# Keys and values of neighbouring units in one load of 64 KB rows

## The chip, the core and the metric

The kernel runs on one core of a Trainium2 chip. The metric is the device time of one execution in microseconds (us), the median of the runs shown. Sizes: 1 MB of a load is 1,048,576 bytes, as the profile counts KB by 1,024; the profile's MB and GB/s are decimal.

## The reference

Two rounds of the same two layers work on one token for each of two batch rows. A layer of attention reads a cache of 4,096 keys and values for 16 heads, and a gated feed-forward layer follows. Everything is float32.

```
B, D, H, Sk, Dh, F = 2, 448, 16, 4096, 256, 1792
def A(x):                                   # attention over the cache
    q = (x @ wq), split into heads          # [B, H, 1, Dh]
    scores = einsum("bhqd,bhkd->bhqk", q, k_cache) * Dh**-0.5
    p = softmax(scores)
    o = einsum("bhqk,bhkd->bhqd", p, v_cache)
    return o, heads joined, @ wo
def F(x):                                   # feed-forward
    gate = x @ W_gate; up = x @ W_up
    return (gate * (gate > 0) * up) @ W_down
x = x + A(layernorm(x)); x = x + F(layernorm(x))
x = x + A(layernorm(x)); x = x + F(layernorm(x))
```

Both rounds use the same weights and the same cache. The cache is 2 x 16 x 4,096 x 256 x 4 bytes, 134 MB for the keys and as much for the values, and it is read once in each round.

## The kernel before, in words

A **unit** is one head of one batch row: 32 units in a pass, and a pass is the attention of one round. A unit's keys are 4,096 rows of 256 floats. They lie on 128 partitions with 32 rows (32 KB) on each, and so do its values. One quarter of that, 8 rows (8 KB) on each partition, 1 MB in all, is a **chunk**; a unit has four chunks of keys and four of values.

All loads go through one arena in SBUF, 27 places of a chunk's size. The first 24 are six blocks of four (`BLOCKS`, line 25), three are single places, mostly for the weights of a head ("h": query weights and output weights, 896 KB) and of the feed-forward layer ("in", "out"). `Arena.take` (line 42) chooses free places: for a load of four chunks the first block that is wholly free, for a single chunk a place that splits no free block.

The order of the loads is a list made before anything runs. `loads` (line 142) puts for each unit the keys, then the values of the unit before, and after each second unit the weights of the next head. `grouped` (line 157) makes one load of 4 MB out of four chunks in mid-pass, with rows of 32 KB; the last 12 entries of a pass (`ENDS`) and the first 25 of the second (`SMALL`) stay single chunks of 1 MB with rows of 8 KB. The first pass goes through the units forwards, the second backwards, so that what is loaded last in the first pass can stay for the second (`keep`, line 171: 20 chunks, one more and one head). `pump` (line 111) takes loads from the head of the list as long as `take` finds a place and issues them at line 125 from the sync engine SP; `release` (line 135) gives a place back and calls `pump`. As the list is strict, a load that finds no place holds up all behind it, and SP takes its waits in that order.

What is done with the data of unit u, in the loop of line 502:

- VectorE multiplies the keys with the query in two halves (`score_block`, line 364, 4,096 elements a partition each) and sums most of them up (line 373); ScalarE sums the first chunk (line 369). All four chunks of the keys are released behind that. Units kept for the second pass go by line 405, chunk by chunk, and so do units 0 to 4 of the second pass, with line 396.
- GpSimd takes the maximum over the partitions (line 416), ScalarE makes the exponentials (line 424).
- In the next turn of the loop TensorE weighs the values (`weigh`, line 443, 32 matmuls a unit) and releases them chunk by chunk. Ahead of it in TensorE's program stand the output projection of the unit pair before (`project`, line 486, which releases the head's weights) and, in odd units, the query of the next pair (`query`, line 323).

So turn u of the loop reads the keys of u and the values of u - 1.

Of the kernel before, what the change touches and what calls it, by code (L numbers as in the profile page):

```python
# [8 lines left out]
F32 = mybir.dt.float32  # L9
# [5 lines left out]
B, D, H, S, DH, F = 2, 448, 16, 4096, 256, 1792  # L15
P = 128
DC = 5
FULL, TAIL = 3, 64
NT = S // P
CT = 8  # L20
UNIT = CT * DH
NC = NT // CT
BLOCKS, SINGLES = 6, 3
KEPT = 20

SUMS = 96
# [9 lines left out]
class Arena:  # L36


    def __init__(self):
        self.free = set(range(BLOCKS * NC + SINGLES))  # L40

    def take(self, n, kind, after=None):

        blocks = [range(NC * i, NC * i + NC) for i in range(BLOCKS)]
        whole = [r for r in blocks if all(k in self.free for k in r)]
        split = {k for r in whole for k in r}
        if n > 1:
            found = [r[0] for r in whole]  # L50
        else:
            found = sorted(self.free, key=lambda k: (k in split, k))
            if kind in "kv":
                found = [k for k in found if k < BLOCKS * NC]
                if after is not None and after % NC != NC - 1 and after + 1 in found:
                    found = [after + 1]
            else:
                single = [k for k in found if k >= BLOCKS * NC]
                found = single if kind == "h" else single + found
        if not found:  # L60
            return None
        self.free -= set(range(found[0], found[0] + n))
        return found[0]
# [3 lines left out]
def two_layers(  # L67
    ctx: ExitStack,
    tc: tile.TileContext,
    x: bass.AP,  # L70
    k_cache: bass.AP,
    v_cache: bass.AP,
    w_head: bass.AP,
    w_in: bass.AP,
    w_out: bass.AP,
# [5 lines left out]
    consts = ctx.enter_context(tc.tile_pool(name="consts", bufs=1))  # L81
# [4 lines left out]
    ps_a = ctx.enter_context(tc.tile_pool(name="ps_a", bufs=1, space=PSUM))  # L86
    ps_f = ctx.enter_context(tc.tile_pool(name="ps_f", bufs=2, space=PSUM))

    arena = consts.tile([P, (BLOCKS * NC + SINGLES) * UNIT], F32, name="arena")
    ctx.enter_context(tc.manual_schedule())  # L90


# [3 lines left out]
    at_of = {}  # L96
    blocks = set()

    def source(key, n):
        kind, name, c = key  # L100
        if kind in "kv":
            h, b = name
            rows = (k_cache if kind == "k" else v_cache)[b, h]
            return rows.rearrange("(p t) d -> p (t d)", t=NT)[:, c * UNIT : (c + n) * UNIT]
        if kind == "h":
            return w_head[name]
        if kind == "in":
            return w_in[c]
        return w_out[:, 14 * P * c : min(14 * P * (c + 1), 14 * D)]

    def pump():
        while pending:
            (kind, name, c), n = pending[0]
            last = at_of.get((kind, name, c - 1)) if kind in "kv" else None
            at = units.take(n, kind, last)
            if at is None:
                return
            pending.pop(0)
            src = source((kind, name, c), n)
            dst = arena[:, at * UNIT : at * UNIT + src.shape[1]]  # L120
            parts = [0, src.shape[1]]
            if not pending:
                parts[1:1] = [src.shape[1] - CLOSE * TAIL]
            for i, j in zip(parts, parts[1:]):
                nc.sync.dma_start(dst[:, i:j], src[:, i:j])
            for k in range(n):
                at_of[kind, name, c + k] = at + k
            if n == NC:
                blocks.add((kind, name))

    def get(*key):
# [3 lines left out]
    def release(*key):  # L135
        units.free.add(at_of.pop(key))
        pump()

    first = [(h, b) for h in range(H) for b in range(B)]
    second = first[::-1]  # L140

    def loads(order):
        found = [("h", order[0][0], 0)]
        for u, unit in enumerate(order):
            found.append(("k", unit, 0))
            if u > 0:
                found.append(("v", order[u - 1], 0))
            if u % 2 and u + 1 < len(order):
                found.append(("h", order[u + 1][0], 0))
        return found + [("v", order[-1], 0)]  # L150

    def cut(found):

        for kind, name, c in found:
            yield from ((kind, name, c + k) for k in range(NC if kind in "kv" else 1))

    def grouped(keys, begin, end):

        keys = list(keys)
        found, i = [], 0  # L160
        while i < len(keys):
            kind, name, c = keys[i]
            whole = kind in "kv" and c == 0 and begin <= i and i + NC <= len(keys) - end
            found.append((keys[i], NC if whole else 1))
            i += found[-1][1]
        return found

    ffn_loads = [("in", "", c) for c in range(7)] + [("out", "", c) for c in range(4)]
    of_first, of_second = list(cut(loads(first))), list(cut(loads(second)))

    keep = {of_second[0], *[key for key in of_second if key[0] != "h"][:KEPT]}
    keep.add(("v", second[2], NC - 1))
    of_second = [key for key in of_second if key not in keep]

    heads = [key for key in of_second if key[0] == "h"][:2]
    of_second = [key for key in of_second if key not in heads]
    of_second[NC - 1 : NC - 1] = heads
    pending += grouped(of_first, 0, ENDS) + [(key, 1) for key in ffn_loads]
    pending += grouped(of_second, SMALL, ENDS) + [(key, 1) for key in ffn_loads]

    row = consts.tile([P, 2 * DH], F32, name="row")
    down = consts.tile([P, D], F32, name="down")
    junk = down[:, :DH]
    y_end_row = row[SUMS : SUMS + B, D:]
    nc.scalar.dma_start(row[:B, :D], x.rearrange("b s d -> (b s) d"))
    pump()


# [557 lines left out]
    found = out.rearrange("b s d -> (b s) d")  # L746
# [11 lines left out]

def _arrays(np, A_x, A_k_cache, A_v_cache, A_wq, A_wo, B_W_gate, B_W_up, B_W_down, **_):

    rows = FULL * P
    wq = A_wq.reshape(D, H, DH)
    head = [wq[c * P : (c + 1) * P].transpose(1, 0, 2) for c in range(FULL)]
    head.append(wq[rows:].reshape(TAIL, H, 2, P).transpose(1, 2, 0, 3).reshape(H, P, P))
    wo = A_wo.reshape(H, 2, P, D)
    head += [wo[:, 0], wo[:, 1]]
    full = [w[c * P : (c + 1) * P] for w in (B_W_gate, B_W_up) for c in range(FULL)]
    full.insert(FULL, np.concatenate([B_W_gate[rows:], B_W_up[rows:]]))
    down = B_W_down.reshape(4, D, D)
    chunks = [down[j, m * P : (m + 1) * P] for j in range(4) for m in range(FULL)]  # L770
    chunks += [np.concatenate([down[j, rows:], down[j + 1, rows:]]) for j in (0, 2)]
    found = {
        "x": A_x,
        "k_cache": A_k_cache,
        "v_cache": A_v_cache,
        "w_head": np.concatenate(head, axis=2),
        "w_in": np.stack(full),
        "w_out": np.concatenate(
            [c[:, at : at + P] for at in range(0, D, P) for c in chunks], axis=1
        ),  # L780
    }
    return {n: np.ascontiguousarray(a) for n, a in found.items()}


def build(nc, shapes):
    import concourse.tile as _tile

    args = [
        nc.dram_tensor(f"in_{n}_dram", s, F32, kind="ExternalInput").ap() for n, s in shapes.items()
    ]  # L790
    for i, (shape, _) in enumerate(_OUTS):
        args.append(nc.dram_tensor(f"out_{i}_dram", shape, F32, kind="ExternalOutput").ap())
    with _tile.TileContext(nc) as tc:
        two_layers(tc, *args)
# [12 lines left out]
```

## Time and profile before

| | |
|---|---|
| runs (us) | 1330.64, 1327.22, 1329.90; median 1329.9 |
| span of the profiled execution, first to last instruction | 1325.7 us |
| median less the profiled span | 4.2 us |
| VectorE busy | 1004.0 us, 76% |
| TensorE busy, matmuls | 581.5 us, 44% |
| ScalarE, GpSimd busy | 325.1 us, 106.2 us |
| moved by all queues | 563.20 MB, 425 GB/s on average |

The profile shows one execution. Its span does not hold what lies ahead of the first and behind the last instruction; the profiled execution's own time isn't listed apart from its span, so the span is set against the median of the three runs.

How to read the rows that follow: a row of a timeline has its start, its length in us, engine and line, output and input, and in brackets how long the engine was idle before and on whom it waited. A row of the DMA issues has the count of loads, the KB of each and the median time from issue to landing. The row of GB/s cuts the span in 40 slices of 33.1 us.

### The profile page before, as it was taken

Reading aid. Unit: us, or ns where it says so; the run is one execution under the profiler, and the core shown is the slowest. Engines: PE = TensorE matmul, PEld = TensorE weight load, DVE = VectorE, ACT = ScalarE, POOL = GpSimd, SP = SyncE. Lnnn points to the kernel's source line nnn. Section 1 sums busy time; section 2 is a strip of 40 time slices with the busy share of each in tenths; the row PEclk is TensorE's granted clock in tenths of the full one; section 3 lists DMA queues with packets and bytes.
Section 4 is the critical chain, followed back from the end, with each engine's and each line's share of the span. In section 5 each row is a group of like instructions: output and inputs, shape, how many; then the busy total and the mean of one; then the engine's idle time right before and its main releaser. Section 6 shows DMA issues by size and latency. Waiting matters only on the chain.

```text
span 1325.7 us, 9957 instructions
## 1 busy us (share of the span) xinstructions
PE 581.5 (44%) x3260; PEld 195.1 (15%) x3260; DVE 1004.0 (76%) x892; ACT 325.1 (25%) x1392; POOL 106.2 (8%) x192
## 2 busy tenths in 40 slices
PE   2434434344343443444584544435345343343438
PEld 2111111111111111111141111111111111111113
DVE  4997877878778787786729888877878778777791
ACT  2221221212212122120026532221212212222131
POOL 0130000000000000000001131000000000000000
PEclk9666566666776766667698677666566665766669
DMA  9999999999999999999999999999999999999997
GB/s 404 429 430 432 429 428 436 426 434 428 430 434 430 432 430 431 431 430 428 417 373 421 428 433 429 434 428 433 429 430 431 430 432 428 434 430 432 429 418 326
DMA packets 30590, 563.20 MB, mean 425 GB/s; under 512 B 3400, under 2 KB 3532, under 8 KB 10316
## 3 DMA queue, kind: packets, MB, share of 16 engines
q1 hardware_dynamic: 30532, 562.58, 99.5%
q8 instruction: 25, 0.41, 0.1%
q14 instruction: 25, 0.20, 0.0%
q10 hardware_dynamic: 8, 0.00, 0.0%
HBM read 562.56 MB, written 0.00 MB: 424 GB/s over the span
## 4 chain that ended last, share of the span: by engine, by line
DMA 68%; DVE 21%; PE 7%; issue 1%; ACT 1%; POOL 1%; DVEq 0%; SPq 0%; POOLq 0%; ACTq 0%
DMA arena<-in_k_cache_dram 50%; DMA arena<-in_w_head_dram 16%; DVE arena L364 10%; DVE scores L373 5%; DVE arena L396 2%; DVE arena L405 2%; DMA arena<-in_v_cache_dram 2%; PE pq L323 1%; PE pf L551 1%; PE acc L486 1%; PE po L443 1%; DVE row L459 1%; DVE scores L402 1%; POOL top L416 1%; ACT arena L398 1%
## 5 line engine op out<-in xcount | busy, mean ns | idle before, releaser
L364 DVE TENSOR_TENSOR arena<-arena 128x4096 f32<-128x4096 f32 x104 | 459.7, 4420 | 210.6 <-DMA arena<-in_k_cache_dram 210.6
L443 PE MATMUL po<-arena,probs 128*2 128x512 f32 x2048 | 316.0, 763 | 106.2 <-DMA arena<-in_v_cache_dram 98.9
L373 DVE TENSOR_REDUCE scores<-arena 128x24 f32<-128x6144 f32 x54 | 352.8, 6534 | 0.0
L467 PE MATMUL small<-ri,row 128*128 128x1 f32 x256 | 62.8, 349 | 460.5 <-DVE row L459 460.5
L369 ACT ACTIVATE arena<-arena 128x256 f32<-128x256 f32 x432 | 173.3, 402 | 290.9 <-DVE arena L364 290.9
L467 PEld LDWEIGHTS small<-ri,row 128*128 128x128 f32 x256 | 57.4, 312 | 520.8 <-DVE row L459 520.8
L421 ACT ACTIVATE nm<-top,nsr 128x1 f32<-128x1 f32 x64 | 18.9, 295 | 372.6 <-POOL top L416 372.6
L443 PEld LDWEIGHTS po<-arena,probs 128*2 128x2 f32 x2048 | 55.7, 98 | 314.3 <-issue 305.3
L486 PE MATMUL acc<-arena,oT 128*2 128x448 f32 x128 | 51.5, 903 | 111.5 <-DVE oT L476 111.5
L416 POOL PARTITION_ALL_REDUCE top<-mx x64 | 50.9, 796 | 611.2 <-DVE mx L414 610.1
L323 PE MATMUL pq<-arena,xs 128*33 128x256 f32 x174 | 75.9, 604 | 42.0 <-DMA arena<-in_w_head_dram 42.0
L369 ACT ACTIVATION_READ_ACCUMULATOR arena<-arena 128x1 f32 x432 | 80.8, 187 | 0.0
L339 POOL PARTITION_BROADCAST arena<-arena x58 | 27.7, 547 | 501.6 <-ACT arena L335 488.7
L335 ACT ACTIVATE arena<-pq 33x256 f32<-33x256 f32 x29 | 10.9, 377 | 203.8 <-PE pq L327 203.8
L459 DVE SCALAR_TENSOR_TENSOR row<-po,lead,row 128x256 f32<-128x256 f32 x64 | 30.7, 480 | 26.5 <-ACT row L456 26.2
L398 ACT ACTIVATE arena<-arena 128x256 f32<-128x256 f32 x97 | 39.0, 404 | 17.6 <-DVE arena L396 17.4
L456 ACT ACTIVATE row<-po,lead 128x256 f32<-128x256 f32 x64 | 29.6, 462 | 51.7 <-PE po L443 51.7
L323 PEld LDWEIGHTS pq<-arena,xs 128*33 128x33 f32 x174 | 25.4, 162 | 111.0 <-issue 96.5
L428 POOL PARTITION_ALL_REDUCE total<-rs x64 | 28.4, 443 | 61.7 <-ACT probs L424 61.7
L405 DVE SCALAR_TENSOR_TENSOR down<-arena,pq 128x256 f32<-128x256 f32 x64 | 26.9, 420 | 8.3 <-DMA arena<-in_k_cache_dram 6.3
L396 DVE TENSOR_TENSOR arena<-arena 128x1024 f32<-128x1024 f32 (+1 forms) x20 | 32.8, 1641 | 0.0
L327 PE MATMUL pq<-arena,xs 128*33 128x128 f32 x116 | 27.6, 384 | 0.0
(144 smaller groups left out, 351.0 us busy)
## 6 DMA issues: line engine op xcount, KB each, us to landing
arena<-in_k_cache_dram SPq DMA_DIRECT2D x56, 4096.0 KB, 45.1
arena<-in_v_cache_dram SPq DMA_DIRECT2D x55, 4096.0 KB, 53.4
arena<-in_w_head_dram SPq DMA_DIRECT2D x31, 896.0 KB, 42.0
arena<-in_v_cache_dram SPq DMA_DIRECT2D x27, 1024.0 KB, 19.8
arena<-in_k_cache_dram SPq DMA_DIRECT2D x20, 1024.0 KB, 16.4
arena<-in_w_in_dram SPq DMA_DIRECT2D x14, 896.0 KB, 19.2
arena<-in_w_out_dram SPq DMA_DIRECT2D x6, 896.0 KB, 9.6
arena<-in_w_out_dram SPq DMA_DIRECT2D x1, 448.0 KB, 8.8
```

The costliest lines, as they stand in the source:

```text
L323: nc.tensor.matmul(q, xs[:, c, :], w[:, c * DH : (c + 1) * DH], start=(c == 0), stop=False)
L364: nc.vector.tensor_mul(some, some, q_of[u][:, None, :].to_broadcast([P, 2 * CT, DH]))
L369: nc.scalar.activation(kt[:, t, :], kt[:, t, :], AF.Copy, accum_out=s_of[u][:, t : t + 1])
L373: nc.vector.reduce_sum(s_of[u][:, CT:], kt[:, CT:, :], axis=AX.X)
L396: nc.vector.tensor_mul(some, some, q_of[u][:, None, :].to_broadcast([P, whole, DH]))
L398: nc.scalar.activation(kt[:, t, :], kt[:, t, :], AF.Copy, accum_out=found[:, t : t + 1])
L405: nc.vector.scalar_tensor_tensor(junk if kept else kt[:, t, :], kt[:, t, :], 1.0, q_of[u], op0=ALU.mult, op1=ALU.mult, accum_out=found[:, ...
L416: nc.gpsimd.partition_all_reduce(mx_of[u], mx, P, RED.max)
L443: nc.tensor.matmul(po_of[u][32 * t : 32 * t + 2, :], p_of[u][:, n : n + 2], vt[:, 2 * t * DH : (2 * t + 2) * DH], start=(c == 0), stop=(c ...
L459: nc.vector.scalar_tensor_tensor(row[:, :DH], po_of.pop(u)[:, DH:], lead[:, 1:2], row[:, :DH], op0=ALU.mult, op1=ALU.add,)
L467: nc.tensor.matmul(pT_of[u][:, c : c + 1], row[:, c * P : (c + 1) * P], r_of[u], start=True, stop=True,)
L486: nc.tensor.matmul(acc[at : at + B], oT_of[h][:, c, :], wo[:, c * D : (c + 1) * D], start=(n < 3), stop=(n >= n_u - 3),)
```

## The change

Keys and values are handed in as one array, `vk`, with a row for each unit and partition: 32 KB of the former unit's values, then 32 KB of the unit's keys, 64 KB in all (former in the order of the first pass; the first unit has the last one's values). For units 1 to 27 of the first pass and at places 9 to 26 of the second pass, one load takes whole rows: 128 rows of 64 KB, 8 MB, the keys of a unit and the values of the one before it. All other loads keep their sizes but find their rows at a step of 64 KB in place of 32 KB.

The arena has the same 27 places, now as three blocks of eight, whose halves serve loads of 4 MB. A pair needs a whole free block of eight; `take` fills the most split places first.

In the second pass the first four units come as before, last to first (31, 30, 29, 28). The other 28 come forwards, 0 to 27, so that the former unit is the one that lies beside the keys in HBM.

The core of the diff:

```diff
-BLOCKS, SINGLES = 6, 3
+BLOCKS, SINGLES = 3, 3
+PAIR = 2 * NC
+WHOLE_FIRST = range(1, 28)
+WHOLE_SECOND = range(9, 27)
...
-        blocks = [range(NC * i, NC * i + NC) for i in range(BLOCKS)]
-        whole = [r for r in blocks if all(k in self.free for k in r)]
-        split = {k for r in whole for k in r}
+        split = {}
+        for size in (NC, PAIR):
+            for i in range(0, BLOCKS * PAIR, size):
+                if all(k in self.free for k in range(i, i + size)):
+                    split |= {k: size for k in range(i, i + size)}
+        found = sorted(self.free, key=lambda k: (split.get(k, 1), k))
         if n > 1:
-            found = [r[0] for r in whole]
+            found = [k for k in found if split.get(k, 1) >= n and k % n == 0]
...
-            rows = (k_cache if kind == "k" else v_cache)[b, h]
-            return rows.rearrange("(p t) d -> p (t d)", t=NT)[:, c * UNIT : (c + n) * UNIT]
+            at = (h * B + b + (kind == "v")) % (H * B)
+            c += NC * (kind == "k" and n < PAIR)
+            return vk[at, :, c * UNIT : (c + n) * UNIT]
...
-                at_of[kind, name, c + k] = at + k
-            if n == NC:
+                key = (kind, name, c + k)
+                if n == PAIR:
+                    key = ("k", name, k - NC) if k >= NC else ("v", behind[name], k)
+                at_of[key] = at + k
+            if n >= NC:
                 blocks.add((kind, name))
...
-    second = first[::-1]
+    second = first[-1:-5:-1] + first[:-4]
+    behind = dict(zip(first[1:], first))
...
         for u, unit in enumerate(order):
-            found.append(("k", unit, 0))
-            if u > 0:
-                found.append(("v", order[u - 1], 0))
+            if u in whole:
+                found.append((("k", unit, 0), PAIR))
+            else:
+                some("k", unit)
+                if u > 0:
+                    some("v", order[u - 1])
             if u % 2 and u + 1 < len(order):
-                found.append(("h", order[u + 1][0], 0))
+                found.append((("h", order[u + 1][0], 0), 1))
...
-        "k_cache": A_k_cache,
-        "v_cache": A_v_cache,
+        "vk": np.concatenate([np.roll(pairs(A_v_cache), 1, 0), pairs(A_k_cache)], axis=2),
```

`some` adds the four chunks of a unit to the list one by one; `grouped` then joins them to loads of 4 MB by the same two bounds as before, where they aren't in a pair.

More of the change, by code (lines that the diff above doesn't have):

```diff
@@ L39, in __init__ @@
     def __init__(self):
-        self.free = set(range(BLOCKS * NC + SINGLES))
+        self.free = set(range(BLOCKS * PAIR + SINGLES))
     def take(self, n, kind, after=None):
-        blocks = [range(NC * i, NC * i + NC) for i in range(BLOCKS)]
-        whole = [r for r in blocks if all(k in self.free for k in r)]
-        split = {k for r in whole for k in r}
-        if n > 1:
-            found = [r[0] for r in whole]
-        else:
[L52 to L59, printed above, removed]
+        split = {}
[4 more added lines that the diff above has]
+        found = sorted(self.free, key=lambda k: (split.get(k, 1), k))
+        if n > 1:
+            found = [k for k in found if split.get(k, 1) >= n and k % n == 0]
+        elif kind in "kv":
+            found = [k for k in found if k < BLOCKS * PAIR]
+            if after is not None and after % NC != NC - 1 and after + 1 in found:
+                found = [after + 1]
+        else:
+            single = [k for k in found if k >= BLOCKS * PAIR]
+            found = single if kind == "h" else single + found
         if not found:
@@ L70, in two_layers @@
     x: bass.AP,
-    k_cache: bass.AP,
-    v_cache: bass.AP,
+    vk: bass.AP,
     w_head: bass.AP,
@@ L87, in two_layers @@
     ps_f = ctx.enter_context(tc.tile_pool(name="ps_f", bufs=2, space=PSUM))
-    arena = consts.tile([P, (BLOCKS * NC + SINGLES) * UNIT], F32, name="arena")
+    arena = consts.tile([P, (BLOCKS * PAIR + SINGLES) * UNIT], F32, name="arena")
     ctx.enter_context(tc.manual_schedule())
@@ L139, in two_layers @@
     first = [(h, b) for h in range(H) for b in range(B)]
-    second = first[::-1]
-    def loads(order):
-        found = [("h", order[0][0], 0)]
-        for u, unit in enumerate(order):
-            found.append(("k", unit, 0))
-            if u > 0:
-                found.append(("v", order[u - 1], 0))
-            if u % 2 and u + 1 < len(order):
-                found.append(("h", order[u + 1][0], 0))
[L150 to L155, printed above, removed]
@@ L157, in grouped, with loads, some @@
-    def grouped(keys, begin, end):
-        keys = list(keys)
-        found, i = [], 0
[L161 to L165, printed above, removed]
+    second = first[-1:-5:-1] + first[:-4]
+    behind = dict(zip(first[1:], first))
+    def loads(order, whole):
+        found = [(("h", order[0][0], 0), 1)]
+        def some(kind, unit):
+            found.extend(((kind, unit, c), 1) for c in range(NC))
+        for u, unit in enumerate(order):
+            if u in whole:
[4 more added lines that the diff above has]
+                    some("v", order[u - 1])
+            if u % 2 and u + 1 < len(order):
+                found.append((("h", order[u + 1][0], 0), 1))
+        some("v", order[-1])
+        return found
@@ L166, in grouped @@
+    def grouped(some, begin, end):
+        found, i = [], 0
+        while i < len(some):
+            (kind, name, c), n = some[i]
+            if n == 1 and kind in "kv" and c == 0 and begin <= i and i + NC <= len(some) - end:
+                n = NC
+            found.append(((kind, name, c), n))
+            i += 1 if n == PAIR else n
         return found
     ffn_loads = [("in", "", c) for c in range(7)] + [("out", "", c) for c in range(4)]
-    of_first, of_second = list(cut(loads(first))), list(cut(loads(second)))
@@ L171, in two_layers @@
-    keep = {of_second[0], *[key for key in of_second if key[0] != "h"][:KEPT]}
+    of_first, of_second = loads(first, WHOLE_FIRST), loads(second, WHOLE_SECOND)
+    keep = {of_second[0][0], *[key for key, _ in of_second if key[0] != "h"][:KEPT]}
     keep.add(("v", second[2], NC - 1))
-    of_second = [key for key in of_second if key not in keep]
-    heads = [key for key in of_second if key[0] == "h"][:2]
-    of_second = [key for key in of_second if key not in heads]
+    of_second = [(key, n) for key, n in of_second if key not in keep]
@@ L177, in two_layers @@
+    heads = [(key, n) for key, n in of_second if key[0] == "h"][:2]
+    of_second = [part for part in of_second if part not in heads]
     of_second[NC - 1 : NC - 1] = heads
@@ L759, in _arrays, with pairs @@
 def _arrays(np, A_x, A_k_cache, A_v_cache, A_wq, A_wo, B_W_gate, B_W_up, B_W_down, **_):
+    def pairs(cache):
+        return cache.transpose(1, 0, 2, 3).reshape(H * B, P, NT * DH)
     rows = FULL * P
```

## The prediction

> **What bounds the kernel now.** I read the page first: the span, the slices, the queues and the chain that ended last. Then I read the DMA issues, and the timelines of VectorE, TensorE and the sync queue in a few steady stretches and at the ends of the passes.
>
> ```profile
> span 1325.7 us, 9957 instructions
> ...
> DMA  9999999999999999999999999999999999999997
> GB/s 404 429 430 432 429 428 436 426 434 428 430 434 430 432 430 431 431 430 428 417 373 421 428 433 429 434 428 433 429 430 431 430 432 428 434 430 432 429 418 326
> ...
> q1 hardware_dynamic: 30532, 562.58, 99.5%
> ...
> DMA 68%; DVE 21%; PE 7%; issue 1%; ACT 1%; POOL 1%; DVEq 0%; SPq 0%; POOLq 0%; ACTq 0%
> ```
>
> The DMA engines are busy in every slice, queue 1 fills 99.5% of their time, and the chain is 68% DMA. The kernel runs at the pace of 562.58 MB through one queue. A change can help by moving the bytes at a better rate or by filling the few slices that dip (417, 373, 421 between the passes, 326 at the end). It can hurt by letting the queue run dry.
>
> ```profile
> 213.14 4.42 DVE L364 TENSOR_TENSOR arena<-arena 128x4096 f32<-128x4096 f32 x1 [5.71 <-DMA arena<-in_k_cache_dram]
> 222.35 6.53 DVE L373 TENSOR_REDUCE scores<-arena 128x24 f32<-128x6144 f32 x1
> 228.98 0.19 DVE L414 TENSOR_REDUCE mx<-scores 128x1 f32<-128x32 f32 x1
> 232.47 4.43 DVE L364 TENSOR_TENSOR arena<-arena 128x4096 f32<-128x4096 f32 x1 [3.30 <-DMA arena<-in_k_cache_dram]
> 254.18 4.43 DVE L364 TENSOR_TENSOR arena<-arena 128x4096 f32<-128x4096 f32 x1 [5.68 <-DMA arena<-in_k_cache_dram]
> 273.50 4.43 DVE L364 TENSOR_TENSOR arena<-arena 128x4096 f32<-128x4096 f32 x1 [3.29 <-DMA arena<-in_k_cache_dram]
> ```
>
> Each L364 row that waited for a key load marks the landing of that load. VectorE works 16.0 us on a unit (213.14 to 229.17) and then waits 3.3 or 5.7 us. So landings set the period. From 213.14 to 232.47 passed 19.33 us, from 254.18 to 273.50 19.32: 4.19 MB of keys and 4.19 MB of values, that is 8.389 MB at **434 GB/s**. With a head's weights (0.918 MB) between, 232.47 to 254.18, it is 21.71 us, so a head costs 2.38 us, which is only 385 GB/s.
>
> **What the change does to the stream.** In mid-pass it replaces two loads of 128 rows of 32 KB by one of 128 rows of 64 KB.
>
> ```profile
> arena<-in_k_cache_dram SPq DMA_DIRECT2D x56, 4096.0 KB, 45.1
> arena<-in_v_cache_dram SPq DMA_DIRECT2D x55, 4096.0 KB, 53.4
> arena<-in_w_head_dram SPq DMA_DIRECT2D x31, 896.0 KB, 42.0
> arena<-in_v_cache_dram SPq DMA_DIRECT2D x27, 1024.0 KB, 19.8
> arena<-in_k_cache_dram SPq DMA_DIRECT2D x20, 1024.0 KB, 16.4
> ```
>
> Units 1 to 27 of the first pass and 9 to 26 of the second give 27 + 18 = 45 pairs. They take the place of 90 of these 111 loads of 4 MB; 21 stay, and so do the 47 loads of 1 MB and the heads. A load is 128 rows on 16 engines, 8 rows and one completion packet on each. Two loads of 4 MB are 18 packets an engine, a pair is 9. Over 45 pairs 45 x 9 x 16 = 6,480 packets go: 30,532 should become 24,052. The bytes stay.
>
> What is a packet worth? The trace has no 64 KB row, so I bound it by the loads with other row lengths.
>
> ```profile
> 662.92 0.11 PEld L443 LDWEIGHTS po<-arena,probs 128*2 128x2 f32 x7 [0.39 <-DMA arena<-in_v_cache_dram]
> 665.42 0.11 PEld L443 LDWEIGHTS po<-arena,probs 128*2 128x2 f32 x8 [1.17 <-DMA arena<-in_v_cache_dram]
> ```
>
> Two chunks of 1 MB (rows of 8 KB) land 2.50 us apart, 419 GB/s. Four of them are 10.00 us and 36 packets an engine; a load of 4 MB is half of 19.33, so 9.67 us and 9 packets. The 27 packets between cost 0.33 us, 12 ns each. At that price a pair saves 9 x 12 = 0.11 us, and 45 pairs **5.0 us**. The head (rows of 7 KB, 9 packets) gives another price. With the byte rate and the packet price from head and 4 MB load together (2.38 = 0.918 MB / r + 9 p; 19.33 = 8.389 MB / r + 18 p) p is 38 ns, and 45 pairs would save 15 us. The lower end is nothing, if the engines are already held by the bytes alone; a loss is bounded under stride below.
>
> The price of a packet falls as rows grow: 38 ns where the 7 KB row enters, 12 ns between 8 and 32 KB. It has no reason to stay at 12 beyond 32 KB, and the 32 KB landings show no more than 0.01 us of spread in these intervals, which looks more like a limit than like a sum of small delays. I take the middle between nothing and 12 ns, nearest to the 32 KB row: 0.055 us a pair, 45 x 0.055 = **2.5 us**, and keep 0 and 5.0 as the ends.
>
> [...]
>
> **What moves besides.** Keys now land together with the former unit's values, 9.67 us later in the stream than they did, and a buffer of 8 MB comes free only when both halves are read. Whether that costs anything is a question of the queue: it runs dry if the next load is issued after the last one in flight has landed.
>
> ```profile
> 244.48 2.74 PE L323 MATMUL pq<-arena,xs 128*33 128x256 f32 x6 [1.07 <-DMA arena<-in_w_head_dram]
> 247.91 3.61 PE L443 MATMUL po<-arena,probs 128*2 128x512 f32 x32
> 251.59 0.33 SPq L125 DMA_DIRECT2D arena<-in_v_cache_dram  x1
> ```
>
> *Steady state.* There are three buffers of a pair. When unit u's pair lands, u+1 is streaming. Its keys are read 16.0 us later; its values by L443, in an odd unit behind the query of L323, at 251.52, 19.1 us after the landing at 232.47 (in an even one earlier). Then SP issues u+3 into the freed buffer. At that moment u+1 and u+2 still fill 19.33 + 21.71 = 41.0 us. The margin is 22 us. The head's load, which SP takes in order ahead of the pair, waits for L486 in the same unit, before L323, so it isn't the later one. Pairs should show some 43 us from issue to landing.
>
> ```profile
> 38.14 2.77 PE L323 MATMUL pq<-arena,xs 128*33 128x256 f32 x6 [13.35 <-DMA arena<-in_w_head_dram]
> 38.48 0.33 SPq L125 DMA_DIRECT2D arena<-in_v_cache_dram  x1
> 562.79 4.43 DVE L364 TENSOR_TENSOR arena<-arena 128x4096 f32<-128x4096 f32 x1 [3.29 <-DMA arena<-in_k_cache_dram]
> 584.50 4.42 DVE L364 TENSOR_TENSOR arena<-arena 128x4096 f32<-128x4096 f32 x1 [5.68 <-DMA arena<-in_k_cache_dram]
> 603.83 0.43 DVE L405 SCALAR_TENSOR_TENSOR down<-arena 128x256 f32<-128x256 f32 x1 [3.30 <-DMA arena<-in_k_cache_dram]
> 625.51 0.42 DVE L405 SCALAR_TENSOR_TENSOR down<-arena,pq 128x256 f32<-128x256 f32 x1 [6.27 <-DMA arena<-in_k_cache_dram]
> 797.74 6.54 DVE L373 TENSOR_REDUCE scores<-arena 128x24 f32<-128x6144 f32 x1
> 805.34 4.43 DVE L364 TENSOR_TENSOR arena<-arena 128x4096 f32<-128x4096 f32 x1 [0.78 <-DMA arena<-in_k_cache_dram]
> ```
>
> *Start.* The third pair needs the buffer of unit 0's keys, free when SP issues at 38.48. Until then the queue holds pair 2, whose 8.39 MB follow the second head, landed by 38.14: to 57.5. Margin 19 us.
>
> *End of the first pass.* Unit 27's keys landed at 562.79; in the pair they land at 562.79 + 9.67 = 572.5, and VectorE is done with them at 588.5. Unit 28's keys (584.50) then start 4.0 us late and end at 604.5, unit 29's (603.83) 0.7 late, unit 30's (625.51) in time. What waits for unit 28's reads are loads still tens of us from their turn. Behind the last pair of the second pass the same three units follow. Cost nothing; if the cover were gone, the 4.0 us each would be the price.
>
> *Turn to pairs in the second pass.* Free buffers are scattered here: by the rule of `take` the first pair (unit 9) fits only where unit 7's keys and unit 6's values have both been read. Before, that load went out a unit earlier. Unit 7's reduction ends at 804.28; behind unit 8's keys (805.34) its predecessor's values follow to 815.0. This is the smallest margin, 10.7 us.
>
> So nothing dries, the added waits cost nothing on the path, and the sum is minus 2.5 us. The profiled span is 1325.7, and the median of the runs, 1329.9, is 4.2 us above it. The other order of heads changes no count of instructions or bytes. The span becomes 1323.2 and the time **1327.4 us**. In this text same means within 0.3% (4.0 us), about what a measurement of this kernel can tell from no change: 1325.9 to 1333.9.
>
> **The rivals.**
>
> *The full price of the packet* (1324.9): 12 ns hold from 32 to 64 KB as well. For it: the two loads compared come from the same caches. Against it: the falling price.
>
> *The head's price* (1314.6): 38 ns. Against it: the 1 MB rows contradict it already.
>
> *Stride, not row length* (slower). The loads that aren't paired now take their rows with a step of 64 KB. A load of 4 MB used to be one run of HBM and becomes 32 KB out of each 64; the chunks of 1 MB go from 8 KB out of 32 to 8 out of 64. Suppose the 0.33 us that four chunks lose to a whole load come from the gaps and not from the packets. Then 21 loads of 4 MB lose up to 0.33 us each, 6.9 us, the 47 chunks perhaps their 0.08 us over again, 3.9, and the pairs gain nothing: 1329.9 + 10.8 = 1340.7. It outweighs the gain of the forecast as soon as a strided 4 MB load takes over 2.5 / 21 = 0.12 us more than a whole one. Against it: the head's rows lie in one run and are the slowest of all. [...]
>
> *The queue dries* (slower): some buffer comes free over 10.7 us later than I count at the turn, or over 22 in steady state, and each us more is lost in full, there once, here 42 times. If it lost 10 us: 1337.4.
>
> *It doesn't do what it says*: a 64 KB row goes out as two packets. Then only 45 x 16 completion packets go, and the time stays at 1329.9.
>
> **How the numbers follow.** Forecast 0.36, full price 0.26, head's price 0.06, stride 0.20, dry queue 0.07, split rows 0.05. Faster: full and head's price and the better edge of the forecast, 0.32 + 0.04 = 0.36. Slower: the last cases but their mildest, 0.25. Same: 0.39. The forecast's own range is 1324.9 to 1329.9. The full range takes in the full price with 3 us for the scatter (the runs go from 1327.22 to 1330.64), and of stride and dry queue the milder half: 1322 to 1338. Outside are the head's price, 0.06, and some 0.13 of the two slower ones.
>
> **What would show it.** Right: 24,052 packets on the queue, 64 KB rows, pair landings 19.25 to 19.30 us apart without a head, unpaired loads as fast as before, no dip in the slices near 810 us. Packets of some 30,000 show split rows; landings of 19.22 or less the full price. Slices under 410 GB/s at 560 to 640 or 680 to 760 us show stride, and a landing gap of over 25 us a dry queue. I am wrong altogether if 64 KB rows themselves are slower than 32 KB rows.

## The result and the profile after

| | before | after |
|---|---|---|
| median of 8 runs each (us) | 1329.54 | 1325.09 |
| ratio | | 0.997, 95% interval 0.996 to 0.9979 |
| a second measurement, medians of 24 and 10 runs | 1328.09 | 1324.57 |
| ratio there | | 0.9979, 95% interval 0.997 to 0.9988 |
| profiled span | 1325.7 | 1323.5 |

The change makes the kernel faster by 0.2 to 0.3%, 3.5 to 4.5 us. (A ratio is estimated from all runs of both kernels and need not be the quotient of the two medians.) Both intervals exclude that nothing changed; whether the gain is over or under 0.3% stays open.

The page of the changed kernel, in the lines that answer to those shown of before:

```profile
span 1323.5 us, 9898 instructions
...
GB/s 408 434 434 432 426 424 448 433 424 436 426 440 431 432 430 431 436 423 427 418 367 411 429 428 442 434 432 428 434 432 436 426 434 432 430 427 432 429 416 327
...
q1 hardware_dynamic: 24052, 562.57, 99.3%
...
arena<-in_vk_dram SPq DMA_DIRECT2D x21, 4096.0 KB, 40.8
...
arena<-in_vk_dram SPq DMA_DIRECT2D x45, 44.3
```

24,052 packets: each of the 45 pairs goes out as 128 packets of 64 KB. The queue is as full as before (99.3% of the engines' time, before 99.5%), and no slice in mid-pass has a hole. The gain must be in the landings. VectorE's timeline, where a row with brackets waited for a pair to land:

```profile
364.49 4.43 DVE L376 TENSOR_TENSOR arena<-arena 128x4096 f32<-128x4096 f32 x1 [3.27 <-DMA arena<-in_vk_dram]
386.10 4.43 DVE L376 TENSOR_TENSOR arena<-arena 128x4096 f32<-128x4096 f32 x1 [5.58 <-DMA arena<-in_vk_dram]
405.35 4.42 DVE L376 TENSOR_TENSOR arena<-arena 128x4096 f32<-128x4096 f32 x1 [3.22 <-DMA arena<-in_vk_dram]
```

A pair without a head takes 19.25 us here (386.10 to 405.35; most of the others lie between 19.25 and 19.30), with a head 21.61. The two together take 40.86 us, and took 41.04 before (21.71 + 19.33). That is 0.09 us a pair by these rows and 0.08 by the commoner 19.27; 45 pairs make 3.6 to 4 us. Over all landings of the mid-passes the median of two neighbouring periods is 40.90 us, and was 41.05 before: 0.075 us a pair, 3.4 us. The measured difference is accounted for, within what rows of 0.01 us can be read to.

In the profiled executions only 2.2 of it are left. The weighing of the first pass's last values starts its last chunk here at 663.50 (before: 665.42):

```profile
663.50 0.11 PEld L455 LDWEIGHTS po<-arena,probs 128*2 128x2 f32 x8 [1.47 <-DMA arena<-in_vk_dram]
```

So the pass is 1.9 us ahead. But in the feed-forward layer that follows, these rows of the stretches (the number behind the engines is TensorE's granted clock, then DMA share and GB/s), before and after, show a lower clock:

```profile
670.00:676.50 6.50, 6.42 (x47) 2.82 (x48) 1.65 (x10) 1.31 (x2) 0.00 (x0) 0.74 0.65 240
```

```profile
670.00:676.50 6.50, 6.50 (x36) 1.79 (x34) 0.77 (x6) 0.00 (x0) 0.00 (x0) 0.57 0.64 210
```

The 32 matmuls of the first projection, before, after, and in the profiled execution of the second measurement of the changed kernel:

```profile
671.85 4.46 PE L551 MATMUL pf<-arena,xs 128*32 128x448 f32 x32
```

```profile
670.19 5.89 PE L563 MATMUL pf<-arena,xs 128*32 128x448 f32 x32
```

```profile
669.86 4.50 PE L563 MATMUL pf<-arena,xs 128*32 128x448 f32 x32
```

At 0.57 in place of 0.74 the projection ran 1.4 us longer in this one execution, and its end is only 0.24 us ahead (676.15 before, 675.91 after, where the next line of TensorE begins). In the other execution of the same kernel it took 4.50 us, the next line begins at 674.20, 1.95 us ahead of before, and the span is 1322.6 us. One profiled execution does not price a change of 0.3%; the many runs and the repeated intervals do.

### The profile page after: what moved, and what is told of

Its sections match the earlier page's. It is cut to its first block, busy times and chain, and to the rows that moved or that the text cites. A ratio compares the mean times of both kernels' runs of the same rounds, so it can differ in the third digit from the quotient of the medians.

```text
span 1323.5 us, 9898 instructions
## 1 busy us (share of the span) xinstructions
PE 566.3 (43%) x3260; PEld 194.7 (15%) x3260; DVE 1003.8 (76%) x892; ACT 324.6 (25%) x1392; POOL 110.1 (8%) x192
## 3 DMA queue, kind: packets, MB, share of 16 engines
q1 hardware_dynamic: 24052, 562.57, 99.3%
## 4 chain that ended last, share of the span: by engine, by line
DMA 59%; DVE 27%; PE 10%; issue 1%; ACT 1%; POOL 1%; another core or an unknown queue 0%; SPq 0%; DVEq 0%; POOLq 0%; ACTq 0%
DMA arena<-in_vk_dram 59%; DVE arena L376 13%; DVE scores L385 7%; PE po L455 3%; DVE arena L408 2%; DVE arena L417 2%; PE pq L335 2%; PE pf L563 1%; PE acc L498 1%; POOL top L428 1%; DVE row L471 1%; DVE scores L414 1%; ACT arena L410 1%; PE pq L339 0%; PE pf L653 0%
## 5 line engine op out<-in xcount | busy, mean ns | idle before, releaser
L455 PE MATMUL po<-arena,probs 128*2 128x512 f32 x2048 | 304.0, 737 | 17.6 <-DMA arena<-in_vk_dram 9.4
L428 POOL PARTITION_ALL_REDUCE top<-mx x64 | 53.6, 838 | 633.7 <-DVE mx L426 633.7
L436 ACT ACTIVATE probs<-scores,nm,sr 128x32 f32<-128x32 f32 x64 | 26.4, 413 | 2.1
## 6 DMA issues: line engine op xcount, KB each, us to landing
arena<-in_vk_dram SPq DMA_DIRECT2D x45, 44.3
```

What stands on the lines that cost most here:

```text
L428: nc.gpsimd.partition_all_reduce(mx_of[u], mx, P, RED.max)
L455: nc.tensor.matmul(po_of[u][32 * t : 32 * t + 2, :], p_of[u][:, n : n + 2], vt[:, 2 * t * DH : (2 * t + 2) * DH], start=(c == 0), stop=(c ...
```

## The experiments

Three theories were set against each other. P: a packet has a price, and the change sends fewer. D: a load has a price; the change halves the loads too, so the trace alone could not tell it from P. O: the gain is the new order, layout or blocks. Every run below was compared with the kernel before on its own chip.

**All but the pairs.**

```diff
-WHOLE_FIRST = range(1, 28)
-WHOLE_SECOND = range(9, 27)
+WHOLE_FIRST = ()
+WHOLE_SECOND = ()
```

> The changed kernel without its pairs: the array of 64 KB rows, the three blocks of eight and the second pass forwards stay, but all mid-pass loads are 4 MB again (128 rows of 32 KB, a step of 64 KB between rows). Theory P (the gain is fewer packets, about 8 ns each by the pair landings of the changed kernel) and theory D (the gain is fewer loads, about 0.075 us each): the time of before, 1329.5. Theory O (the gain comes from the order, the layout or the blocks): 1325. Stride rival: 111 strided loads of 4 MB cost up to 0.33 us each, so up to 1366.

Measured: 1327.96 us beside 1328.02, ratio 0.9999 (0.9991 to 1.0007). Its landings, with a head and without:

```profile
356.23 4.42 DVE L376 TENSOR_TENSOR arena<-arena 128x4096 f32<-128x4096 f32 x1 [3.30 <-DMA arena<-in_vk_dram]
377.95 4.42 DVE L376 TENSOR_TENSOR arena<-arena 128x4096 f32<-128x4096 f32 x1 [5.69 <-DMA arena<-in_vk_dram]
397.28 4.43 DVE L376 TENSOR_TENSOR arena<-arena 128x4096 f32<-128x4096 f32 x1 [3.30 <-DMA arena<-in_vk_dram]
```

21.72 and 19.33, as before. Theory O falls. So does the rival of the stride: 111 loads of 4 MB take their rows with a step of 64 KB, and landings and time are those of the kernel before, whose loads were whole runs.

**One load, shorter rows.** The pairs come from an array with the row cut in 2, or 8, pieces and 256 bytes between them, so that a piece can't join the next in one packet (29,812 and 64,372 packets went, 128 and 896 a pair more than the changed kernel's 24,052). Load, block and moment of issue stay.

```diff
-            for i, j in zip(parts, parts[1:]):
+            if n == PAIR:
+                some = vk_pieces[name[0] * B + name[1], :, GAP:]
+                some = some.rearrange("p (m w) -> p m w", m=PIECES)[:, :, GAP:]
+                nc.sync.dma_start(dst.rearrange("p (m w) -> p m w", m=PIECES), some)
+                parts = []
+            for i, j in zip(parts, parts[1:]):
```

> The changed kernel with each pair still one load into the same block, but as 256 rows of 32 KB: the two halves of a row lie 256 bytes apart in HBM. 17 packets an engine and pair in place of 9, 24052 + 45 x 128 = 29812 in all. Theory P: 45 x 8 x 8 ns = 2.9 us slower than the changed kernel, 1328. Theory D: as the changed kernel, 1325.1.

> The same with 1024 rows of 8 KB in one load, gaps of 256 bytes: 65 packets an engine and pair in place of 9. Theory P: 45 x 56 x 8 to 12 ns = 20 to 30 us slower than the changed kernel, 1345 to 1355. Theory D: as the changed kernel, 1325.1.

Measured: 1328.67 us with rows of 32 KB (ratio 1.0002, 0.9994 to 1.0011), 1348.12 with rows of 8 KB (1.0146, 1.0133 to 1.0159). The queue and the landings, first with rows of 32 KB, then of 8 KB:

```profile
q1 hardware_dynamic: 29812, 562.57, 99.3%
```

```profile
346.75 4.43 DVE L383 TENSOR_TENSOR arena<-arena 128x4096 f32<-128x4096 f32 x1 [5.65 <-DMA arena<-in_vk_pieces_dram]
366.11 4.43 DVE L383 TENSOR_TENSOR arena<-arena 128x4096 f32<-128x4096 f32 x1 [3.32 <-DMA arena<-in_vk_pieces_dram]
387.78 4.43 DVE L383 TENSOR_TENSOR arena<-arena 128x4096 f32<-128x4096 f32 x1 [5.64 <-DMA arena<-in_vk_pieces_dram]
```

```profile
q1 hardware_dynamic: 64372, 562.57, 99.9%
```

```profile
353.36 4.43 DVE L383 TENSOR_TENSOR arena<-arena 128x4096 f32<-128x4096 f32 x1 [6.13 <-DMA arena<-in_vk_pieces_dram]
373.13 4.42 DVE L383 TENSOR_TENSOR arena<-arena 128x4096 f32<-128x4096 f32 x1 [3.75 <-DMA arena<-in_vk_pieces_dram]
395.29 4.43 DVE L383 TENSOR_TENSOR arena<-arena 128x4096 f32<-128x4096 f32 x1 [6.13 <-DMA arena<-in_vk_pieces_dram]
```

Two units take 41.93 us with rows of 8 KB (353.36 to 395.29), 41.03 with 32 KB (346.75 to 387.78), 40.86 with 64 KB (364.49 to 405.35). Two pairs have 96 packets an engine fewer at the first step and 16 at the second. That is 0.90 us / 96 = **9.4 ns** and 0.17 / 16 = **10.6 ns** a packet; 0.01 us in the second difference is 0.6 ns. The medians of two periods over all landings of the mid-passes, 41.94, 41.05 and 40.90 us, give 9.3 and 9.4 ns. So the price is the same at both ends as far as these rows can tell, and the whole gain is undone by packets alone: theory P holds, and D, which expected 1325 of both, falls. The times say the same: 1348.12 less 1328.67 over 45 x 48 packets is 9.0 ns. The gaps of 256 bytes are no cost that shows: the run without pairs, with rows of 32 KB and no gap, has 41.05 us for two units, and the chunks before, rows of 8 KB without a gap, took 2.50 us for 1 MB, where these rows of 8 KB take 19.77 / 8 = 2.47.

**Twice the loads, the same rows.** First the two halves of the partitions, then the even and the odd ones.

```diff
+            if n == PAIR:
+                for some in (slice(0, P // 2), slice(P // 2, P)):
+                    nc.sync.dma_start(dst[some], src[some])
+                parts = []
```

> The changed kernel with each pair cut in two loads of 64 partitions, rows of 64 KB: the loads of before in number, the long rows of after; 4 data packets and one completion packet an engine in each, 10 a pair in place of 9. Theory P: 45 x 8 ns = 0.4 us slower than the changed kernel, 1325.5. Theory D: 45 x 0.075 = 3.4 us slower, 1328.5.

Measured: 2362.14 us, ratio 1.7765. Neither theory had that in it.

```diff
+            if n == PAIR:
+                for some in range(2):
+                    nc.sync.dma_start(dst[some::2], src[some::2])
+                parts = []
```

> The changed kernel with each pair cut in two loads of 64 partitions as in the run with the halves of the partitions, but the even ones and the odd ones. [...] If any load of 64 partitions runs at half the rate: 2360 us again.

Measured: 1325.20 us beside 1328.09, ratio 0.9977 (0.9968 to 0.9987); the changed kernel on the same chip had 0.9979, and theory D, at 0.075 us a load, would have these 90 loads 3.4 us slower than its 45. The GB/s of the halves, then of even and odd:

```profile
GB/s 235 213 199 200 208 198 200 209 194 206 207 194 208 206 196 207 199 203 207 199 428 396 413 433 211 208 201 197 207 194 195 209 196 196 207 203 198 300 425 294
```

```profile
GB/s 405 435 437 436 431 414 444 438 429 428 431 437 433 431 435 425 434 426 423 420 363 418 427 434 436 437 434 429 429 429 437 433 436 424 425 434 432 428 417 289
```

Where pairs run, the halves move about 200 GB/s, and where loads of 128 partitions run (the middle, from the 21st slice) 396 to 433. Even and odd run at about 430 GB/s with as many loads of as many bytes. So 45 more loads cost nothing that these runs can tell, and which 64 partitions a load has goes with its rate. The two cuts also take different rows of HBM, one run of 4 MB or every other row of 64 KB; but the loads of 4 MB before were single runs too, over 128 partitions, and went at 434 GB/s, so the run in HBM is not what is slow. Why the halves are slow no run here shows.

**Same cut, equal and unequal.** Two loads from one row, 128 partitions each: 32 and 32 KB, or 56 and 8 KB.

```diff
             parts = [0, src.shape[1]]
+            if n == PAIR:
+                parts[1:1] = [7 * UNIT]      # 4 * UNIT for the equal cut
...
```

> The changed kernel with each pair in two loads from the same row of 64 KB: 128 rows of 56 KB, then 128 rows of 8 KB, 18 packets an engine in place of 9. By the packet price alone (9.5 ns): 45 x 9 x 9.5 ns = 3.8 us slower than the changed kernel, as the run with the halves. If each short load among long ones pays some 0.18 us more, as the heads seem to (2.68 us for 1 MB alone, 2.50 for a chunk among chunks): 45 x 0.18 = 8 us more than that, 12 us slower.

> The same cut in two equal loads: 128 rows of 32 KB each, 18 packets an engine; blocks, order and time of issue of the changed kernel. Packet price: 3.8 us slower than the changed kernel, the time of before. If the load and not the packet were paid for: 3.4 us slower as well, but then the run with even and odd partitions should have lost it too, and it did not.

Measured: 1328.20 us (ratio 1.0002, 0.9992 to 1.0011) and 1328.11 (1.0006, 0.9997 to 1.0015), beside 1327.86. Both give the gain back in full, as 9 more packets a pair at 9.5 ns should (3.8 us), and no more. The equal cut and the even and odd partitions are the same 90 loads of 4 MB; with 18 packets an engine and pair the gain is gone, with 10 it stays (1328.11 and 1325.20 us, each beside its own measurement of before). So it is the packets. The short load of 1 MB among long ones pays nothing of its own here.

**What a head's weights cost.** Between the pairs of the changed kernel a head still takes 21.61 - 19.25 = 2.36 us. Byte rate and packets would have it at 2.18: 0.918 MB at the 437 GB/s that are left for the bytes of a pair when 9 packets of 9.5 ns are taken out of its 19.27 us, and 9 packets of its own. The surcharge is 0.18 us, or 0.16 by the commoner landings. Four runs looked for the reason.

```diff
-        "w_head": np.concatenate(head, axis=2),
+        "w_head": np.pad(np.concatenate(head, axis=2), ((0, 0), (0, 0), (0, UNIT - 7 * DH))),
...
-            return w_head[name]
+            return w_head[name, :, : 7 * DH]     # this line only where 7 KB are read
...
```

> The changed kernel with the rows of a head's weights 8 KB apart in HBM in place of 7 KB; 7 KB of each are read as before. The landings of the changed kernel (19.27 us without a head, 21.61 with one) leave 2.34 us for a head. At the byte rate and the packet price of the other loads (437 GB/s, 9 packets of 9.5 ns) it would be 2.18. If the step of 7 KB is the cause: 31 x 0.16 = 5 us less than the changed kernel, 1320 beside its 1325. If it is something else in a short load: as the changed kernel.

> The same, and all 8 KB of each row are read, 1 MB a head, the last 1 KB of it zeros that nothing uses. If rows of 7 KB are slow for their length: a head lands in 2.48 us like a chunk of keys, 31 x 0.14 = 4 us slower than the changed kernel. If 7 KB rows carry no surcharge and the cost is one for each short load: 2.34 + 0.131 MB / 437 GB/s = 2.64, 9 us slower.

Measured: 1324.85 us with the other step (ratio 0.9976, 0.9965 to 0.9986; the changed kernel 0.9979), so the step is not it. With 8 KB read 1334.72 (1.0047, 1.0035 to 1.0059), 10 us more, and these landings:

```profile
366.96 4.43 DVE L376 TENSOR_TENSOR arena<-arena 128x4096 f32<-128x4096 f32 x1 [3.24 <-DMA arena<-in_vk_dram]
388.88 4.42 DVE L376 TENSOR_TENSOR arena<-arena 128x4096 f32<-128x4096 f32 x1 [5.90 <-DMA arena<-in_vk_dram]
408.14 4.43 DVE L376 TENSOR_TENSOR arena<-arena 128x4096 f32<-128x4096 f32 x1 [3.23 <-DMA arena<-in_vk_dram]
```

1 MB costs 21.92 - 19.26 = 2.66 us there. The length of the row is not it either.

```diff
-            dst = arena[:, at * UNIT : at * UNIT + src.shape[1]]
+            dst = arena[:, spot(at) : spot(at) + src.shape[1]]   # spot: single places first
...
```

> The changed kernel with the single places at the front of the arena and the blocks behind them, so that a head's weights land in the first 24 KB of a partition's part and not in the last. If the place in SBUF costs a head its 0.16 us: 31 x 0.16 = 5 us less than the changed kernel, unless the blocks pay for it now. If not: as the changed kernel, 3.5 us below the kernel before.

```diff
-            return w_head[name]
+            return vk[name * B, :, PAIR * UNIT : PAIR * UNIT + 7 * DH]
...
-        "vk": np.concatenate([np.roll(pairs(A_v_cache), 1, 0), pairs(A_k_cache)], axis=2),
+        "vk": np.concatenate([np.roll(pairs(A_v_cache), 1, 0), pairs(A_k_cache), heads], axis=2),
```

> The changed kernel with a head's weights in HBM beside its first unit's pair: rows of 72 KB, of which a pair takes the first 64 KB and the head 7 KB of the rest. Same loads, same packets. If the place in HBM (an array of its own) costs a head its 0.16 us: 31 x 0.16 = 5 us less than the changed kernel. If not: as the changed kernel.

Measured: 1324.39 us (0.9968, 0.9956 to 0.998) and 1323.98 (0.9967, 0.9956 to 0.9977), beside 1329.03. Both are the changed kernel again; neither gains 5 us. For the heads in rows only the times speak: the one execution with a trace took 2428.55 us (last section), so its landings say nothing of the others. Where a head's 0.18 us go stays open: not the step, the length, the place in SBUF or in HBM, nor, by the run with 56 and 8 KB, that it is a short load among long ones.

## Why the prediction was right, and where it wasn't

- *The bound.* Right: landings set the period before and after, and only what makes them quicker counted.
- *The packets.* 24,052 were worked out and 24,052 went.
- *The price of a packet.* Here the working had its failed step: "The price of a packet falls as rows grow", and with it the half of 12 ns. It doesn't fall as far as the rows can tell: 9.4 ns between 8 and 32 KB, 9.4 to 10.6 between 32 and 64. The other reason given, no more than 0.01 us of spread in the 32 KB landings, held for the two intervals shown only: over the mid-passes before, the intervals without a head run from 19.31 to 20.05 us, with a median of 19.33. The 12 ns, which rested on a single interval between two chunks, were too high, the halved 6 too low. 45 x 9 x 9.5 ns are 3.8 us, between the 2.5 of the forecast and the 5.0 of its rival. That the sum came within 2 us of the measured gain is the luck of a middle taken between two wrong prices; nothing in the working led to 9 ns. Of the 2.3 us between the 1327.4 forecast and the 1325.09 measured, 1.3 are this term and 0.4 the starting point (1329.9 from three runs, 1329.54 from eight); the rest is within the scatter of the medians. What seemed to show a falling price was the head, and its surcharge is no packet price at all.
- *The limit.* The working took the small spread of the 32 KB landings for the look of a limit, and its lower end, no gain, was the case of engines held by the bytes alone. Landings of 19.25 to 19.30 us are 435.8 to 434.6 GB/s, above the 434 of before, so the bytes did not hold them there. Whether there is a limit above that no run shows: the packet price alone leads to 19.33 - 0.09 = 19.24.
- *The margins.* Nothing dried. Pairs took 44.3 us from issue to landing, against some 43. At the turn to pairs in the second pass, SP and VectorE of the changed kernel:

```profile
804.35 0.33 SPq L128 DMA_DIRECT2D arena<-in_vk_dram  x1
```

```profile
834.12 4.43 DVE L376 TENSOR_TENSOR arena<-arena 128x4096 f32<-128x4096 f32 x1 [12.95 <-DMA arena<-in_vk_dram]
```

  The first pair was issued at 804.35, when unit 7's reduction ended, and landed at 834.12; 815.0 + 19.3 = 834.3 was the place for it in an unbroken stream. VectorE waited 12.95 us for it, and no transfer did.
- *The late keys.* At the end of the first pass unit 28 starts the moment unit 27 is done, and unit 30 waits for its load again:

```profile
570.28 4.43 DVE L376 TENSOR_TENSOR arena<-arena 128x4096 f32<-128x4096 f32 x1 [3.25 <-DMA arena<-in_vk_dram]
...
586.26 4.43 DVE L376 TENSOR_TENSOR arena<-arena 128x4096 f32<-128x4096 f32 x1
...
623.27 0.42 DVE L417 SCALAR_TENSOR_TENSOR down<-arena,pq 128x256 f32<-128x256 f32 x1 [4.10 <-DMA arena<-in_vk_dram]
```

  The lag is worked off by unit 30, and the pass ends 1.9 us earlier, not later.
- *The rivals.* Stride, split rows and a dry queue are each refuted by a run or a row above; the head's price is refuted as the price of a packet.

## What to carry to other kernels

In a stream that keeps the DMA queue full, count the packets an engine, not the loads: here a packet cost some 9 to 10 ns whatever its length from 8 to 64 KB, and twice the loads for the same rows, cut into even and odd partitions, cost nothing that could be measured (1325.20 us, the changed kernel on that chip 1324.57). A price taken from one odd kind of transfer (here the heads) should not be spread over others until a run varies only the one thing. Joining two streams in one load cost nothing besides in this kernel, where each buffer comes free 10 us and more before the loads in flight have landed; that can be worked out from the issue and landing rows before anything is built.

## What the runs showed of the hardware that was not expected

- Loads to partitions 0 to 63 and then 64 to 127 ran at about 200 GB/s, loads to even and odd partitions at about 430, and the kernel took 2362 us in place of 1325.
- Rows of 32 KB with a step of 64 KB in HBM are read as fast as a whole run: 19.33 us for 8.389 MB either way.
- A head's load costs 0.18 us more than bytes and packets explain, and the same with rows of 8 KB (2.66 us, where byte rate and packets give 2.48).
- One execution of ten of the run with the heads in rows took 2428.55 us, with a span of 2426.5 us and a mean granted clock of TensorE of 1.0. The other nine took 1322.96 to 1327.96 us at 0.664 to 0.687. Nothing measured here shows why.
